# Attention and gated MLP on one core: chunk 0's rows in another order, one load on another queue, and a new instruction planner

## The chip, the core and the metric

The kernel runs on one core of a Trainium2 chip. A core has a matrix engine (TensorE, in the profile PE, with its weight loads as PEld), three engines for elementwise work (VectorE or DVE, ScalarE or ACT, GpSimd or POOL) and SyncE (SP), which only issues transfers. Sixteen DMA engines move data between the DRAM and the on-chip memory. A transfer is issued on the queue of SP, ACT or POOL and all of them share those sixteen. Each engine works through its own instructions in order; an instruction that waits for another engine or for a transfer holds up all that stand behind it. Matmul results land in eight PSUM banks, from which DVE or ACT must read them before the bank can be used again.

The metric is the device time of one execution in microseconds. Before the change it was 222.25 us, the median of three runs (221.79, 222.25, 227.55).

## The reference

Two stages follow each other. Decayed linear attention over q, k, v of 4 batches, 8 heads, 768 positions and 64 channels:

```python
for b in range(nb):                                   # blocks of 64 positions
    intra = einsum('bhic,bhjc->bhij', qb, kb) * Dmask # Dmask[i,j] = lam**(i-j) for i >= j
    intra = einsum('bhij,bhjd->bhid', intra, vb)
    inter = einsum('bhid,bhde->bhie', qb * lam_pow, kv_state)
    out[:, :, sl] = intra + inter
    kv_state = lam_block * kv_state + einsum('bhsd,bhse->bhde', kb * rev_pow, vb)
```

Its output, as x with 3072 rows (batch and position) and 512 columns (head and channel), goes through a layer with a periodic gate, and the result is stored as float32, [3072, 512]:

```python
h = x @ w_in                    # [3072, 2048]
s = sin(alpha * h)
g = h + s * s / (alpha + 1e-9)
return g @ w_out                # [3072, 512]
```

## The kernel before

**Attention.** The kernel uses 24 blocks of 128 rows, six to a batch. Instead of a mask with decay, queries and keys are scaled by powers of lam (tiles Lq, Lp, Lk), so that a 0/1 mask is left. For each block: load q, k, v; scale q and k to bf16 (qk); cast v; transpose the scaled q and k (tile qkT); scores S (L635) and their masked copy Sm on DVE (L646); state Z (L671), copied out as Zd or Zc; output O from the state (L708, L721) and from the scores (L730); copy of O to xT, transposed activations for the next stage (L740). Blocks 0 to 11 are transposed on PE (Q at L561, K at L583, T at L543) and copied out by DVE or ACT; from block 12 on, SP issues a DMA transpose (L534).

**Mixed rows.** Blocks 0 to 3 are loaded so that a partition gets neighbouring rows (q in fours, k and v in pairs), which makes longer runs in DRAM. O of these blocks comes out with its 128 rows sorted by their place within four. The copy to xT (L740) puts them back in order: `xT[...].rearrange("p a (x t) -> p a t x", t=nq)`, a strided write.

**The dense layer.** Rows are worked on in six chunks of 512. `unit_A` (four matmuls of 512 columns, L779) and `unit_A2` (eight of 256, L813) compute h for a slice of 128 columns into a bank. ACT takes the sine (t, L789 or L823), POOL or ACT squares it (u, L794, L793, L828, L827), DVE forms u * rinv + h (gT, L796 or L831). `unit_B` (four matmuls, L844) adds up four slices of the second product; after four of them ACT copies the bank to osb (L857) and a transfer stores 128 rows (L859). Chunk 0's four stores go out on SP's queue, all others but the very last on ACT's.

**Start.** `lam` (decay rates) and `alphaT` are loaded on ACT's queue; SP issues q, k, v of blocks 0 to 3 and the first slices of w_in. ACT computes ln(lam) (L460), then the powers (L464 to L470), with a table load ahead of each new kind of function, and then loads the table for the sine (L471). alpha is transposed by PE (L474), copied by DVE (L476), and aeps and rinv follow at once on DVE. Until the first unit_A, filler matmuls on a constant tile (`spin`, L935, 512 columns) stand in PE's gaps. Of the first scalings, DVE does two products of q and one of k, POOL two of q (L495) and three of k (L513).

**The planner.** The order of instructions on each engine is not written by hand. The kernel records operations with an engine (or a choice of engines), a planned duration, and what they read and write; `_Plan._order` then lays them out in planned time, and `emit` issues them with semaphore waits. `_order` always takes the operation that can start first, by planned durations; a fixed 0.2 us (LAT) is added between engines, PE may choose among the next 40 of its operations and SP none. A transfer is planned with an issue time, a time on the wire and a latency; `_transfers` shares the wire among the queues, and `_settle` repeats the plan eight times with the landings of the last pass and keeps the one that agrees best. `P.lead` moves attention pieces ahead in the priorities.

SP's order around chunk 0's stores: loads of blocks 10 and 11, the four stores, loads of blocks 12 and 13, loads of block 14, transpose of block 12, the loads of k and v of block 15, transpose of block 13, and so on.

Of the kernel before, what the change touches and what calls it, by code (L numbers as in the profile page):

```python
# [5 lines left out]
ALU = mybir.AluOpType  # L6
# [7 lines left out]
class _Op:  # L14


    def __init__(self, eng, emit, dur, reads, writes, dma, after, issue, lat, runs=64):
        self.eng, self.emit, self.dur = eng, emit, dur
        self.given = eng
        self.issue, self.lat, self.runs = issue, lat, runs  # L20
        self.lead = 0
# [11 lines left out]
class _Plan:  # L33

    AHEAD = {"PE": 40, "SP": 1}
    SLACK = 0.3  # L40
    EARLY = 0.0, 0.0

    LAT = 0.2
# [10 lines left out]
    def op(self, eng, emit, dur, reads=(), writes=(), dma=None, after=(), issue=0.4, lat=2.6, runs=64):  # L54
# [14 lines left out]
        o.deps.discard(o)  # L69
        o.lead = self.lead  # L70
# [4 lines left out]
    def _transfers(order):  # L75
# [5 lines left out]
        left = {e: [[o.start + 0.8, o.runs, o.dur / o.runs, o] for o in sorted(q, key=lambda o: o.start)]  # L81
# [19 lines left out]
    def _settle(self):  # L101

        filler, lands, best = self.filler, {}, None
        for _ in range(8):
            self.filler = filler
            for o in self.ops:
                o.eng, o.start, o.done = o.given, None, None
            order = self._order(lands)
            new = self._transfers(order)
            off = sum(abs(t - o.done) for o, t in new.items())  # L110
            state = [(o, o.eng, o.start, o.done) for o in order]
            if best is None or off < best[0]:
                best = off, order, state
# [5 lines left out]
    def _order(self, lands):  # L119
        index = {o: i - o.lead for i, o in enumerate(self.ops)}  # L120
        left = {}
        for o in self.ops:
            left.setdefault(o.eng if isinstance(o.eng, str) else "any", []).append(o)
        fixed = {e: left.pop(e, []) for e in ("PE", "SP")}
        free = [o for e in left for o in left[e]]
        clock = {e: 0.8 for e in ("PE", "SP", "ACT", "DVE", "POOL")}
        wire = 0.0
        port = 0.0
        order = []

        def ready(o):
            t = 0.0
            for d in o.deps:
                if d.done is None:
                    return None
                t = max(t, d.done + (0.0 if d.eng == o.eng else self.LAT))
            return t

        while fixed["PE"] or fixed["SP"] or free:
            best = None  # L140
            for e in ("PE", "SP"):
                can = []
                for o in fixed[e][:self.AHEAD[e]]:
                    r = ready(o)
                    if r is not None:
                        can.append((max(r, clock[e]), index[o], o, e, o.dur))
                if can:
                    soon = min(c[0] for c in can)
                    soon += self.EARLY[1] if e == "PE" and soon < self.EARLY[0] else self.SLACK
                    c = min((c for c in can if c[0] <= soon), key=lambda c: c[1])  # L150
                    if best is None or c[:2] < best[:2]:
                        best = c
            for o in free:
                r = ready(o)
                if r is None:
                    continue
                if o.port:
                    r = max(r, port)
                if isinstance(o.eng, str):
                    c = (max(r, clock[o.eng]), index[o], o, o.eng, o.dur)  # L160
                else:
                    _, e, d = min((max(r, clock[e]) + d + late, e, d) for e, d, late in o.eng)
                    c = (max(r, clock[e]), index[o], o, e, d)
                if best is None or c[:2] < best[:2]:
                    best = c
            t, _, o, e, dur = best
            if e == "PE" and self.filler is not None:
                emit, reads, last = self.filler
                if last.start is not None:
                    self.filler = None  # L170
                else:
                    deps = [self.writer[b] for b in reads]
                    at = max([clock["PE"]] + [d.done + self.LAT if d.done is not None else t for d in deps])
                    n = int((t - at) / 0.4)
                    if n > 0:
                        f = _Op("PE", lambda h, n=n: emit(h, n), 0.4 * n, tuple(reads), (), None, (), 0, 0)
                        f.deps = set(deps)
                        f.start, f.done = at, at + 0.4 * n
                        order.append(f)
            if isinstance(o.eng, str):  # L180
                (fixed[e] if e in fixed else free).remove(o)
            else:
                free.remove(o)
                o.eng = e
            o.start = t
            if o.dma is not None:
                clock[e] = t + o.issue
                wire = max(wire, t + 0.8) + dur
                o.done = max(t + 0.8 + o.dur + o.lat, lands[o]) if o in lands else wire + o.lat
            else:  # L190
                clock[e] = o.done = t + dur
                if o.port and e != "ACT":
                    port = o.done
            order.append(o)
        return order
# [48 lines left out]
def bass_lightning_attn__then__act_snake_kernel(  # L244
# [34 lines left out]
    QD = ((0, 0), (1, 0))  # L279

    es = contextlib.ExitStack()
    with es:
# [51 lines left out]
        def _(_unused_eng):  # L334
# [562 lines left out]
            for i in range(1, 4):  # L897
                load_w1(i, [last["v32", 1]])
# [137 lines left out]
```

## Time and profile before

| | us |
|---|---|
| median of three runs | 222.25 |
| the three runs | 221.79, 222.25, 227.55 |
| the profiled execution | 221.06 |
| its span | 219.2 |
| PE, ACT, DVE, POOL busy | 207.6, 157.2, 123.0, 96.0 |
| filler matmuls L935 | 8.4 |
| first matmul of the dense layer (L813) | starts at 20.58 |
| last store lands | end of the span |

The times of the runs are those of executions without the profiler; the profile is of one execution, and its own time is the span plus the parts ahead of it and behind it. A line such as `L646 DVE TENSOR_TENSOR Sm<-bank,mask 128x1024 bf16<-128x1024 f32 x24 | 29.1, 1222 | 10.4` reads: line, engine, operation, output and inputs, shape and type, number of instructions, then their time in us and the mean of one in ns, and the idle time of the engine just ahead of them. In rows by time the first two numbers are the start and the duration in us; "x4" says that four instructions are merged. SPq and ACTq are issues of transfers on the queues of SP and ACT. "To landing" is the time from the start of an issue to the last byte. Matmuls overlap, so a matmul of 512 columns is listed with 0.38 us, while four of them follow each other in 0.86 us. The "DMA" row gives the mean busy share of the sixteen DMA engines in 40 slices; in the tables by stage it can pass 1, as one engine can have more than one packet under way.

### The profile page before, as it was taken

What the parts mean: (1) busy time and instruction counts of PE and PEld (TensorE: products, weight loads), DVE (VectorE), ACT (ScalarE), POOL (GpSimd) and SP (SyncE); (2) the same over time, 40 slices, a digit from 0 to 9 for tenths busy, and PEclk for the clock granted to TensorE, in tenths of its full rate; (3) what the DMA queues carried; (4) which work ended last, traced back from release to release, by engine and by line L of the source; (5) the groups of instructions that cost most, each with busy time, mean ns of one, the idle gap of its engine ahead of it and who ended that gap; (6) DMA issues with size and microseconds to landing.
All of it is one profiled execution on the core that took longest, in us unless ns stands there. A gap on an engine that the chain in (4) does not pass through costs nothing.

```text
span 219.2 us, 4238 instructions
## 1 busy us (share of the span) xinstructions
PE 207.6 (95%) x1714; PEld 112.2 (51%) x1739; DVE 123.0 (56%) x185; ACT 157.2 (72%) x279; POOL 96.0 (44%) x110
## 2 busy tenths in 40 slices
PE   7787999999999979999999999999999999999995
PEld 2365544446577656555445444545544444444454
DVE  4688675444878858957564556545464544444100
ACT  4577986364988888969798787878778677777221
POOL 7793677756886777574551533011001011110100
PEclk9999999999999999999999999999999999999999
DMA  4999999999999999999999560110011011101212
GB/s 132 310 314 210 207 215 214 220 219 250 235 314 221 240 186 271 162 290 179 281 254 208 123 144 10 41 48 35 16 48 51 0 48 48 51 0 48 87 58 96
DMA packets 78499, 33.31 MB, mean 152 GB/s; under 512 B 55296, under 2 KB 75536, under 8 KB 78480
## 3 DMA queue, kind: packets, MB, share of 16 engines
q1 hardware_dynamic: 71728, 24.25, 53.4%
q0 software_dynamic: 3696, 3.67, 10.1%
q10 hardware_dynamic: 3056, 5.13, 6.5%
q8 instruction: 13, 0.21, 0.4%
q14 instruction: 6, 0.05, 0.1%
HBM read 27.28 MB, written 6.29 MB: 153 GB/s over the span
## 4 chain that ended last, share of the span: by engine, by line
PE 66%; DMA 20%; POOL 5%; ACT 3%; DVE 2%; issue 2%; SPq 1%; ACTq 0%; POOLq 0%
PE bank L844 33%; PE bank L779 22%; DMA k<-in_k_dram 10%; PE bank L813 4%; DMA w<-in_moe_w_in_dram 4%; DMA q<-in_q_dram 3%; DMA v<-in_v_dram 3%; PE bank L730 2%; PE bank L635 2%; POOL qk L513 2%; SPq L346 1%; POOL u L794 1%; POOL qk L505 1%; PE bank L708 1%; DVE gT L831 1%
## 5 line engine op out<-in xcount | busy, mean ns | idle before, releaser
L844 PE MATMUL bank<-w,gT 128*128 128x512 bf16 (+1 forms) x382 | 91.3, 371 | 1.8 <-issue 1.3
L796 DVE SCALAR_TENSOR_TENSOR gT<-u,rinv,bank 128x512 bf16<-128x512 bf16 x74 | 54.6, 745 | 52.2 <-ACT u L793 30.0
L779 PE MATMUL bank<-xT,w 128*128 128x512 bf16 x290 | 73.1, 379 | 0.6 <-issue 0.2
L789 ACT ACTIVATE t<-bank,alpha 128x512 bf16<-128x512 f32 x74 | 50.5, 686 | 23.2 <-PE bank L779 23.1
L794 POOL TENSOR_TENSOR u<-t 128x512 bf16<-128x512 bf16 x26 | 26.9, 1039 | 86.6 <-ACT t L789 84.7
L844 PEld LDWEIGHTS bank<-w,gT 128*128 128x128 bf16 x400 | 37.9, 98 | 39.5
L779 PEld LDWEIGHTS bank<-xT,w 128*128 128x128 bf16 x296 | 28.5, 98 | 34.1 <-ACT xT L740 0.6
L646 DVE TENSOR_TENSOR Sm<-bank,mask 128x1024 bf16<-128x1024 f32 x24 | 29.1, 1222 | 10.4 <-PE bank L671 7.1
L793 ACT ACTIVATE u<-t 128x512 bf16<-128x512 bf16 x48 | 30.0, 628 | 1.3
L857 ACT COPY osb<-bank 128x512 f32<-128x512 f32 (+1 forms) x25 | 14.2, 571 | 14.3 <-PE bank L844 14.2
L505 POOL TENSOR_TENSOR qk<-q,Lq 128x512 bf16<-128x512 f32 x20 | 20.4, 1042 | 8.2 <-DMA q<-in_q_dram 8.2
L813 PE MATMUL bank<-xT,w 128*128 128x256 bf16 x176 | 22.5, 273 | 1.5 <-DVE gT L831 1.5
L525 POOL TENSOR_TENSOR qk<-k,Lk 128x512 bf16<-128x512 f32 x20 | 20.8, 1042 | 2.6 <-DMA k<-in_k_dram 2.5
L823 ACT ACTIVATE t<-bank,alpha 128x256 bf16<-128x256 f32 x44 | 18.5, 474 | 4.5 <-PE bank L813 4.1
L831 DVE SCALAR_TENSOR_TENSOR gT<-u,rinv,bank 128x256 bf16<-128x256 bf16 x44 | 18.8, 474 | 4.9 <-ACT u L827 2.6
L813 PEld LDWEIGHTS bank<-xT,w 128*128 128x128 bf16 x176 | 16.1, 98 | 4.8 <-DVE gT L831 2.4
L740 ACT CAST xT<-bank 128x512 bf16<-128x512 f32 (+1 forms) x18 | 14.4, 799 | 3.6 <-PE bank L671 2.2
L528 ACT CAST v<-v 128x512 bf16<-128x512 f32 x16 | 9.8, 614 | 4.3 <-DMA v<-in_v_dram 4.3
L828 POOL TENSOR_TENSOR u<-t 128x512 bf16<-128x512 bf16 x9 | 9.3, 1038 | 6.5 <-ACT t L823 6.5
L730 PE MATMUL bank<-Sm,v 128*64 128x128 bf16 (+1 forms) x224 | 11.0, 224 | 0.6 <-DVE Sm L646 0.3
L635 PE MATMUL bank<-qkT 64*128 64x128 bf16 (+1 forms) x224 | 9.6, 219 | 0.3 <-ACT qkT L594 0.2
L935 PE MATMUL bank<-idle 128*128 128x512 bf16 x21 | 8.4, 540 | 1.6 <-DVE idle L441 1.5
(68 smaller groups left out, 125.7 us busy)
## 6 DMA issues: line engine op xcount, KB each, us to landing
q<-in_q_dram SPq DMA_DIRECT2D x12, 512.0 KB, 5.6
k<-in_k_dram SPq DMA_DIRECT2D x24, 256.0 KB, 5.5
v<-in_v_dram SPq DMA_DIRECT2D x24, 256.0 KB, 5.7
out_dram<-osb ACTq DMA_DIRECT2D x19, 256.0 KB, 2.0
w<-in_moe_w_out_dram POOLq DMA_DIRECT2D x4, 512.0 KB, 12.7
w<-in_moe_w_in_dram POOLq DMA_DIRECT2D x3, 512.0 KB, 8.0
ws<-in_moe_w_in_dram SPq DMA_DIRECT2D x2, 512.0 KB, 6.2
out_dram<-osb SPq DMA_DIRECT2D x4, 256.0 KB, 4.2
```

The source lines that it names most:

```text
L505: lambda e, a=a: e.tensor_tensor(qk2[:, j:j + 2, 4 * a:4 * a + 4, :], q32[:, jq, 4 * a:4 * a + 4, :, :].rearrange("p h t d -> p t h d"), b ...
L525: lambda e: e.tensor_tensor(qk2[:, j, H:2 * H, :], block32(k32, jl), lk, ALU.mult), 1.05,
L646: op("DVE", lambda e: e.tensor_tensor(Sm[js][:, :, :], banks[:, 512 * b0:512 * b0 + 1024].rearrange("p (c i) -> p c i", i=128), bass.AP(ma ...
L779: ins = e.matmul(ps[hb][:, c0:c1], w1[:, kc, 128 * m:128 * (m + 1)], xT[x][:, kc, c0:c1], start=(kc == 0 and c0 == lo), stop=(kc == NKC - ...
L789: op("ACT", lambda e: e.activation(t16[ju][:, w], ps[hb][:, w], ACTF.Sin, scale=alpha[:, m:m + 1]), 0.69 * f, [bank(hb), "alpha"], [("t16" ...
L793: lambda e: (e.activation(u16[ju][:, w], t16[ju][:, w], ACTF.Square) if e is nc.scalar else e.tensor_tensor(u16[ju][:, w], t16[ju][:, w], ...
L794: e.tensor_tensor(u16[ju][:, w], t16[ju][:, w], t16[ju][:, w], ALU.mult)), 0,
L796: op("DVE", lambda e: e.scalar_tensor_tensor(out=gT[g][:, m, w], in0=u16[ju][:, w], scalar=rinv[:, m:m + 1], in1=ps[hb][:, w], op0=ALU.mul ...
L813: ins = e.matmul(ps[hb][:, 256 * i:256 * i + 256], w1[:, kc, 128 * (m + i):128 * (m + i + 1)], xT[x][:, kc, lo:lo + 256], start=(kc == 0 a ...
L823: op("ACT", lambda e, i=i: e.activation(t16[ju][:, 256 * i:256 * i + 256], ps[hb][:, 256 * i:256 * i + 256], ACTF.Sin, scale=alpha[:, m + ...
L831: op("DVE", lambda e, i=i: e.scalar_tensor_tensor(out=gT[g][:, m + i, lo:lo + 256], in0=u16[ju][:, 256 * i:256 * i + 256], scalar=rinv[:, ...
L844: ins = e.matmul(ps[ob][:, w], gT[g][:, m, 128 * s4:128 * (s4 + 1)], w2[:, m, w], start=(m == 0), stop=(m == NM - 1),)
```

## The change

1. **Rows of blocks 0 to 3.** The copy to xT writes them in the order in which they lie in the bank, a contiguous write; the rows of a block are put in order by the store of chunk 0, whose pattern in DRAM is then 4 x 32 rows of 512 instead of 128 rows of 512.
2. **Start.** lam is loaded on SP's queue, ahead of q. alpha is copied from its bank by ACT instead of DVE; aeps and rinv are recorded later. DVE does all four products of q and three of the four of k; POOL does one of k. Of the four value casts, ACT does that of blocks 2 and 3, first half, instead of blocks 0 and 1, first half. The filler matmul has 256 columns instead of 512, and scores of block 3 are recorded ahead of the output of block 0.
3. **Planner.** `_order` is rewritten: each engine has a window within which the priority decides (WINDOW), an overlap of consecutive instructions (PIPE), a delay after another engine's work (HOP, and DRAIN after PE), and fillers have two durations. Many planned durations and transfer times are new. Engines and orders of most of the program change with it.

```diff
-    AHEAD = {"PE": 40, "SP": 1}
-    SLACK = 0.3
-    EARLY = 0.0, 0.0
-    LAT = 0.2
+    AHEAD = 40
+    WINDOW = {"PE": 0.3, "ACT": 0.1, "DVE": 0.1, "POOL": 0.1}
+    PIPE = {"ACT": 0.11, "DVE": 0.09, "POOL": 0.045, "PE": 0.0}
+    HOP = {"PE": 0.055, "ACT": 0.035, "DVE": 0.035, "POOL": 0.075, "SP": 0.1}
+    DRAIN = 0.085
+    MOVES = ()
+    SPIN = 0.22, 0.11, 7.4
...
-    QD = ((0, 0), (1, 0))
+    QD = ((0, 0), (0, 2), (1, 0), (1, 2))
...
-            load(lam_bc[:, :], ..., "lam", 0.1, "lam", "ACT", runs=1)
+            load(lam_bc[:, :], ..., "lam", 0.1, "lam", "SP", lat=1.3, runs=1)
...
-            op("DVE", lambda e: e.tensor_copy(alpha[:, :], ps[4][:, 0:NM]), 0.2, [bank(4)], ["alpha"])
-            op("DVE", lambda e: e.tensor_scalar_add(aeps[:, :], alpha[:, :], 1e-9), 0.2, ["alpha"], ["aeps"])
-            op("DVE", lambda e: e.reciprocal(rinv[:, :], aeps[:, :]), 0.2, ["aeps"], ["rinv"])
+            op("ACT", lambda e: e.copy(alpha[:, :], ps[4][:, 0:NM]), 0.2, [bank(4)], ["alpha"])
...
-                        eng, dur = (("DVE", 0.9) if a == 0 else ("POOL", 1.05)) if s == 0 else ("POOL", 1.05)
+                        eng, dur = ("DVE", 0.66) if s + a < 3 else ("POOL", 1.05)
...
-                        op("ACT" if s + a == 0 else "POOL", ...
+                        op("ACT" if s and not a else "POOL", ...
...
-                        xT[c % RX][:, a0:a1, BL * i4:BL * (i4 + 1)].rearrange("p a (x t) -> p a t x", t=nq),
+                        xT[c % RX][:, a0:a1, BL * i4:BL * (i4 + 1)].rearrange(
+                            "p a (x t) -> p a t x" if s >= 4 else "p a (t x) -> p a t x", t=nq),
...
-                    op(eng, lambda e: e.dma_start(out[row:row + 128, w], osb[jo][:, w]), 0.75,
+                    rows = out[row:row + 128, w] if c else bass.AP(out.tensor, row * DM + lo, [[DM, 4], [4 * DM, 32], [1, hi - lo]])
+                    op(eng, lambda e: e.dma_start(rows, osb[jo][:, w]), 0.75,
...
-            piece_O(0, 3)
             piece_S(3, 5, 6)
+            piece_O(0, 3)
...
-                    ins = e.matmul(ps[0][:, :], idle[:, 0:128], idle[:, :])
+                    ins = e.matmul(ps[0][:, 0:256], idle[:, 0:128], idle[:, :])
```

The new loop that takes the next operation:

```python
for e, c in per.items():                       # c: (earliest start, priority, op, duration)
    if not c:
        continue
    soon = min(x[0] for x in c) + self.WINDOW.get(e, 0.0)
    x = min((x for x in c if x[0] <= soon), key=lambda x: (x[1], num[x[2]]))
    if best is None or x[0] < best[0]:
        best = x[0], x[2], e, x[3]
```

More of the change, by code (lines that the diff above doesn't have):

```diff
@@ L101, in _settle @@
     def _settle(self):
[L103 to L111, printed above, removed]
+        prio = {o: i - o.lead for i, o in enumerate(self.ops)}
+        for at, width, kind, by in self.MOVES:
+            for o in self.ops[at:at + width]:
+                if (kind == "all" and o.given != "SP") or o.given == kind or (kind == "any" and not isinstance(o.given, str)):
+                    prio[o] += by
+        lands, best = {}, None
+        for _ in range(10):
+            order, new, off = self._pass(prio, lands)
             if best is None or off < best[0]:
-                best = off, order, state
+                best = off, order, [(o, o.eng, o.start, o.done) for o in order]
+            if off < 0.5:
+                break
             lands = new
@@ L117, in _settle, with _pass @@
         return best[1]
[L119 to L121 removed]
+    def _pass(self, prio, lands):
         for o in self.ops:
[L123 to L168 removed]
@@ L194, in _order @@
             order.append(o)
+            can.discard(o)
+            left -= 1
+            for s in after.get(o, ()):
+                waits[s] -= 1
+                if not waits[s]:
+                    can.add(s)
         return order
```

166 lines of the change are left out of this document (110 added, 56 removed).

## The prediction

> **What bounds the kernel now.** I read the busy shares and the slices first, then the list of waits for TensorE (PE) alone, then the order of time on single engines around the places where PE stops. The page of the profile:
>
> ```profile
> PE 207.6 (95%) x1714; PEld 112.2 (51%) x1739; DVE 123.0 (56%) x185; ACT 157.2 (72%) x279; POOL 96.0 (44%) x110
> ...
> DMA  4999999999999999999999560110011011101212
> ...
> q1 hardware_dynamic: 71728, 24.25, 53.4%
> ...
> q10 hardware_dynamic: 3056, 5.13, 6.5%
> ```
>
> PE is busy for 95% of the span, but its first 20 us are partly filler matmuls (L935), and the DMA engines are full until about 118 us. So there are two limits: PE from the first real matmul of the dense part (20.58 us) on, and before 118 us the transfers that feed it. The waits of PE (engine, line, what it waited for: total us, times, longest):
>
> ```profile
> PE bank L813 <- DVE gT L831: 1.5, 2, 1.2
> ...
> PE bank L543 <- POOL qk L525: 0.5, 1, 0.5
> ```
>
> Between 20.58 us and the end these are nearly all that PE loses: 0.48 us at 41.27 (keys of block 4 not yet scaled, their load landed at 40.01), 0.26 at 59.09 and 1.20 at 79.71 (gate values late, behind a value cast that waited on ACT for its load), 0.16 at 97.95. Together 2.1 us: a better order can win no more there. The third view is the SP queue and the attention of block 12, the first block whose transposes are DMAs (start us, us, engine, line):
>
> ```profile
> 59.39 2.83 SPq L859 DMA_DIRECT2D out_dram<-osb  x4
> 62.26 0.84 SPq L346 DMA_DIRECT2D q<-in_q_dram  x1
> ...
> 73.09 3.31 SPq L534 DMA_TRANSPOSE qkT<-qk  x1
> ...
> 77.69 2.27 SPq L534 DMA_TRANSPOSE qkT<-qk  x1
> ```
> ```profile
> 85.86 0.40 PE L635 MATMUL bank<-qkT 64*128 64x128 bf16 x8
> ```
>
> The four stores of chunk 0 stand in the same queue right ahead of the loads of blocks 12 and 13 (from 62.26). The transposes of those blocks go out at 73.09 and 77.69; the second landed 4.4 us later, at 82.1. The scores of block 12 need both and start at 85.86: 3.7 us of slack.
>
> **Part by part: the start.** Decay rates on SP: one more issue of 0.44 us with its gap (0.47) ahead of all loads, so k lands 0.47 later (9.19 to 9.66); between 0 and 0.47, I take 0.47 and cost it at nothing, because the products below start later still (without that cover, +0.47). The rates themselves landed 3.5 us after their issue; from SP, with nothing ahead, between 1.7 (the shortest landing in the trace, the last store) and 3.5; I take 3.5, because they start the engines' work together with the same loads. More weighs that the copy of alpha is now on ACT, ahead of the table load for the exponentials:
>
> ```profile
> 4.59 1.28 ACT L464 ACT_TABLE_LOAD   x1
> 5.88 0.23 ACT L464 ACTIVATE Lq<-lnL 128x32 f32<-128x32 f32 x1
> ...
> 15.79 1.31 ACT L740 CAST xT<-bank 128x512 bf16<-128x512 f32 x1 [0.23 <-PE bank L730]
> ```
>
> alphaT, first on its queue, lands 3.5 us (lam's time there) to 4.8 us (its own) after 0.81, at 4.3 to 5.6. PE transposes it behind 18 half-size fillers (half of 0.43 us each, from 1.5: 5.3), 0.23 us, then the copy, 0.2: ACT is free at 5.8 to 6.1 instead of 4.57, and Lq is there at 7.3 to 7.6 instead of 6.11. Queued behind this wait: the four exponentials, and all scaling. DVE now does four q and three k products, 0.66 us each (L495 on DVE) where POOL took 1.29 and 1.23. From 7.4 the sixth ends at 11.4, against 11.04 in before, so the first scores start at 12.6 instead of 12.24: +0.4. If POOL's one k product runs beside a DVE one, that costs up to 0.9 more (the DVE one of before that ran beside POOL took 1.52). Sin's table load hides in ACT's idle time, and the changed value casts (0.61 us on either engine) wait for later loads.
> The four mask products (4.62 us in a row) shift with the scores. Against that, the contiguous xT copies: 1.31 us becomes 0.74 (a later L740 copy of that size, at 74.31), and two of them stand in ACT's chain Zd, xT, Zd that ends at O(3): up to 1.1 back. The dense part starts at 19.9 to 21.0; I take 20.3, **-0.3 us**. Smaller filler and idle tiles, and the move of aeps and rinv, change nothing on the path: DVE waits for Lq there anyway.
>
> **The planner.** I counted, in the two programs' orders on PE, how many dense units (four 512-column or eight 256-column matmuls, 0.864 us) precede each attention piece. Block 4's key transposes move from 22 to 25, blocks 8 to 11 by 3 to 4 units back: the waits at 41.27 and 79.71 lose their cause. I take 1.0 of the 2.1 us, since new small waits of that kind are as likely as old ones go: **-1.0**; bounds 0 and -2.1. Against the stream the scores of block 12 come *forward* from 56 to 54, block 14 from 67 to 65, block 16 from 79 to 75; from 85 on the orders agree. Forward by 1.73 us leaves block 12 2.0 us of slack, and block 14 1.7 (transposes landed 93.2, use at 96.61). 22 squares move from POOL to ACT (61 to 83), 0.63 us each, 13.9 us on an engine with 62 us idle; hidden while ACT keeps up (second rival).
>
> **The store.** Chunk 0's rows are permuted by the store: its DRAM pattern changes from 128 rows to 4 x 32 rows. The packet count says how a transfer is dealt out: q10's 3056 packets are 20 stores of 128 rows, 128 for lam, 16 for alphaT, and 352 = 22 transfers x 16. So every transfer there closed with 16 packets, which I read as 16 shares, one for each DMA engine, alphaT with its 16 rows among them. Every pattern in before has 128 or 16 as its outermost size; the new one has 4. I forecast that the outermost size sets the shares: **four engines instead of 16**. The trace can't decide it: 16 rows fit "always 16" as well.
> Price: q10 moved 5.13 MB in 6.5% of 16 x 219.2 us, 22.5 GB/s for one engine. Four stores of 256 KB are 64 KB per engine on 16 (2.9 us), but 256 KB on each of four (11.6 us). Those four engines fall 8.7 us behind, and each later load on this queue, spread over all, ends with them. Between 64 and 74 us the DMA share is 0.84 to 1.09, against about 1.25 when full: some 2.2 us to catch up (five windows of 2 us). So the transposes of block 13 land 6.5 us late, at 88.6 (bounds: 5.0, if the engines go at up to 27 GB/s as the last stores suggest, 256 KB in 2.0 us and 128 KB in 1.7; 8.7 without catching up). PE comes to the scores of block 12 at 85.86 - 1.73 - 1.3 = 82.8 and stands for 5.8 us; everything behind it on PE waits too, the second half of the dense work with it. Blocks 14 and 16 then come after their data, and the loss stays. What is gained ahead only lengthens this wait, so the net loss is lateness less slack, 6.5 - 2.0 = 4.5; down to 1.7, if the first transpose, held at 73.09 by the queue and not by its data (1.3 us), hides that much.
> The Trainium skill, page "DMA: Bandwidth & Descriptors", section "Why a DMA increments its semaphore by 16 and not by 1", speaks against this change: by it the hardware queues take the largest number up to 16 that divides the slowest dimension of both sides. By that rule it is 4 here; no run here shows it yet.
> A stop of over 5 us can also cost speed behind it. At the start fillers of 512 columns stand 0.43 us apart until 7.04, later such matmuls 0.216: a cold spell of 5.9 us, up to 3 us lost. After the 1.20 us wait at 79.71 nothing was slower. I take 0, nearest to the waits seen in mid-kernel, and keep 3.
> By the Trainium skill's "TensorE: Matmul & The Clock Gate", Part 1, an idle window of about 3.4 us halves the clock and a busy one restores it; by that rule the sum would be 1.7 us higher.
>
> **Sum.** 221.06 (span 219.2 and 1.86 around it) - 0.3 - 1.0 + 5.8 = 225.6. The two lower runs shown (221.79, 222.25) lie 0.7 and 1.2 above the profiled one; with 0.9 the forecast is **226.5 us**.
>
> **Rivals.** *All 16 engines carry the store* (not slower): then transposes land at 82.1, ahead of PE at 82.8, and the gains stay: 221.06 - 1.3 = 219.8, as timed 220.6 (219.4 to 221.9); for it, that all 22 transfers of q10 closed with 16 packets. The landing at 82.1 also caps it: beyond 2.0 us of gain PE waits again. *ACT becomes the bound*: between 80 and 120 us ACT is busy 33.7 of 40 us; some five squares more there at 0.57 us (two in a row took 1.14 at 24.95) make 91%, and in-order waits for loads stand among them. If all of that reaches PE: 221.06 - 0.3 + 2.8 = 223.6, as timed 224.5. Against it, ACT waits 23 us for PE at L779. *The change wins nothing at its start* (exponentials late by 1.5, a DVE and POOL collision): +0.4, inside the ranges.
>
> **Chances.** Forecast 0.58, sixteen engines 0.30, ACT 0.12. The forecast's own range is 223.7 to 229.5 (222.8 to 227.6 by the bounds, 0.9 added, some of the 3 us of cold clock); to leave out under 2 in 10 the range takes in the second case: 219.6 to 229.5. Two per cent, about what a measurement of this kernel tells from no change, ends at 217.8 and 226.7. Slower: somewhat under half of the forecast and a bit of ACT, 0.30. Faster: a tenth of the sixteen engines, and planner's luck, 0.04. Same: 0.66.
>
> **What would show it.** q10 must have 2912 packets; q1 71872 with 16 closing packets for each store, 71824 with four. The four stores land in 4.3 to 5.4 us now; with four engines after 8 us and more. PE idles 4 to 7 us at L654 near 83 us, waiting for qkT. Lq near 7.4, the dense part from 20.3, xT copies at 0.74 show the start. Wrong it would be if the stores land as before, or if SP's loads of block 12 do not queue behind them.

## The result and the profile after

| | before | after |
|---|---|---|
| median of the runs | 222.25 us (three runs, as above) | 229.66 us (four runs: 228.13, 229.46, 229.85, 232.41) |
| ratio of after to before, 95% interval | | 1.0294 [1.0227, 1.0361] |
| a second set of after, six runs | 222.87 us (11 runs) | 229.75 us, ratio 1.031 [1.0251, 1.0369] |
| the profiled execution, its span | 221.06, 219.2 us | 232.41, 230.5 us |

The change makes the kernel 3% slower; the forecast was 226.5 us, about 2%. A fourth execution of before took 358.71 us and is left out of its median. The profiled execution of after is the longest of its four, and that of before (221.06) is shorter than all its timed ones, so the traces lie 11.35 us apart where the medians lie 7.4 apart. Ratios here and below leave out single executions that are more than 1.5% above the fastest of their kernel; medians do not.

From the page of after: the clock granted to PE in 40 slices, the busy share of the DMA engines, and the queues (packets, MB, share):

```profile
PEclk9997699999999999599999999999999999999999
DMA  4999999999744899999999618101100111011122
...
q1 hardware_dynamic: 71824, 24.26, 48.7%
...
q10 hardware_dynamic: 2912, 5.12, 6.8%
```

q1 has 71824 packets, the number foretold for four engines (71872 would have been 16). Where before's DMA engines were full, in the slices from 58 to 81 us, they drop to four to eight tenths. And PE, at full clock throughout in before, runs at half clock in two places. The SP queue of after (start, duration), and the waits of PE (total us, times, longest):

```profile
60.15 5.78 SPq L880 DMA_DIRECT2D out_dram<-osb  x4
65.97 0.51 SPq L368 DMA_DIRECT2D q<-in_q_dram  x1
66.53 4.56 SPq L368 DMA_DIRECT2D k<-in_k_dram  x1
71.13 3.62 SPq L368 DMA_DIRECT2D v<-in_v_dram  x1
...
80.91 2.75 SPq L553 DMA_TRANSPOSE qkT<-qk  x1
...
84.95 3.29 SPq L553 DMA_TRANSPOSE qkT<-qk  x1
```
```profile
PE bank L654 <- DMA qkT<-qk: 5.2, 1, 5.2
```

The loads of block 12 stand behind the stores (q for 12 and 13 at 65.97, then k and v of 12). Their issues, 0.8 to 2.6 us each in before, now take up to 4.6 us. The transposes go out at 80.91 and 84.95 instead of 73.09 and 77.69. The second takes 7.5 us to land, at 92.5 (4.4 us, at 82.1, in before). The chain that ended last (start, us, what) runs through just these pieces:

```profile
65.97 10.38 DMA q<-in_q_dram
...
84.95 7.53 DMA qkT<-qk
```

PE stops for 5.2 us ahead of the scores of block 12 (L654), and then works at half clock. The table by stage gives the busy time of each engine, and at the end of the row the clock, the DMA share and GB/s:

```profile
92.53 0.61 PE L654 MATMUL bank<-qkT 64*128 64x128 bf16 x8 [5.20 <-DMA qkT<-qk]
93.07 3.60 PE L833 MATMUL bank<-xT,w 128*128 128x256 bf16 x16
```
```profile
90.00:95.00 5.00, 2.47 (x18) 1.73 (x19) 1.23 (x1) 0.16 (x2) 0.87 (x1) 0.65 1.21 247
95.00:100.00 5.00, 5.00 (x21) 2.50 (x20) 1.22 (x3) 3.89 (x8) 2.17 (x3) 0.67 1.26 233
```

Sixteen matmuls of 256 columns took 3.60 us, against 2.02 for the first sixteen of the dense part in before. By the two rows the half clock lasts (0.35 + 0.33) x 2 x 5 = 6.8 us, to 98.3, and behind the wait it costs (98.3 - 92.5) / 2 = 2.9 us.

The books: block 12's scores start at 92.53. In before they started at 85.86, and the new order has them two dense units (1.73 us) earlier, so they are 8.4 us late. With 2.9 us of clock that makes 11.3, the whole difference of the two profiled executions (232.41 - 221.06 = 11.35). What PE did ahead of that wait is hidden in it.

### The profile page after: what moved, and what is told of

It reads as the page before. It is cut to its first block, busy times and chain, and to the rows that moved or that the text cites. A ratio compares the mean times of both kernels' runs of the same rounds, so it can differ in the third digit from the quotient of the medians.

```text
span 230.5 us, 4320 instructions
## 1 busy us (share of the span) xinstructions
PE 216.3 (94%) x1769; PEld 118.5 (51%) x1769; DVE 119.8 (52%) x182; ACT 167.9 (73%) x307; POOL 69.2 (30%) x85
## 3 DMA queue, kind: packets, MB, share of 16 engines
q1 hardware_dynamic: 71824, 24.26, 48.7%
## 4 chain that ended last, share of the span: by engine, by line
PE 77%; DMA 10%; DVE 5%; ACT 4%; POOL 2%; issue 1%; SPq 0%
PE bank L864 34%; PE bank L799 28%; DMA q<-in_q_dram 7%; PE bank L833 4%; DMA qkT<-qk 3%; PE bank L749 3%; PE bank L654 2%; PE bank L959 2%; POOL qk L524 2%; DVE Sm L665 2%; PE bank L727 1%; DVE qk L532 1%; ACT t L843 1%; DVE gT L851 1%; PE bank L690 1%
## 5 line engine op out<-in xcount | busy, mean ns | idle before, releaser
L864 PE MATMUL bank<-w,gT 128*128 128x512 bf16 (+1 forms) x400 | 95.1, 371 | 0.0
L799 PE MATMUL bank<-xT,w 128*128 128x512 bf16 x296 | 76.0, 386 | 0.0
L799 PEld LDWEIGHTS bank<-xT,w 128*128 128x128 bf16 x296 | 29.3, 99 | 35.3 <-issue 1.4
L813 ACT ACTIVATE u<-t 128x512 bf16<-128x512 bf16 x67 | 42.0, 629 | 2.0
L524 POOL TENSOR_TENSOR qk<-q,Lq 128x512 bf16<-128x512 f32 x20 | 20.4, 1042 | 20.9 <-DMA q<-in_q_dram 20.9
L833 PE MATMUL bank<-xT,w 128*128 128x256 bf16 x176 | 25.7, 300 | 0.5 <-DVE gT L851 0.3
L833 PEld LDWEIGHTS bank<-xT,w 128*128 128x128 bf16 x176 | 17.5, 107 | 5.4 <-DVE gT L851 1.7
L654 PE MATMUL bank<-qkT 64*128 64x128 bf16 (+1 forms) x224 | 9.6, 222 | 6.6 <-DMA qkT<-qk 5.2
L759 ACT CAST xT<-bank 128x512 bf16<-128x512 f32 (+1 forms) x19 | 13.0, 685 | 1.7 <-PE bank L749 1.7
L654 PEld LDWEIGHTS bank<-qkT 64*128 64x128 bf16 (+1 forms) x224 | 5.7, 99 | 11.6 <-DMA qkT<-qk 5.4
L749 PE MATMUL bank<-Sm,v 128*64 128x128 bf16 (+1 forms) x224 | 11.5, 233 | 0.0
L848 POOL TENSOR_TENSOR u<-t 128x512 bf16<-128x512 bf16 x6 | 6.2, 1038 | 16.3 <-ACT t L843 16.3
L814 POOL TENSOR_TENSOR u<-t 128x512 bf16<-128x512 bf16 x7 | 7.3, 1037 | 12.0 <-ACT t L809 12.0
L547 ACT CAST v<-v 128x512 bf16<-128x512 f32 x15 | 9.0, 615 | 2.5 <-DMA v<-in_v_dram 2.4
```

The lines of the kernel that those rows point to most:

```text
L524: lambda e, a=a: e.tensor_tensor(qk2[:, j:j + 2, 4 * a:4 * a + 4, :], q32[:, jq, 4 * a:4 * a + 4, :, :].rearrange("p h t d -> p t h d"), b ...
L654: ins = e.matmul(ps[(b0, b1)[h]][x, 128 * jp:128 * (jp + 1)].rearrange("p (t x) -> p t x", t=nq), qkT[r, jt, 4 + jp, x], qkT[r, jq:jq + nq ...
L799: ins = e.matmul(ps[hb][:, c0:c1], w1[:, kc, 128 * m:128 * (m + 1)], xT[x][:, kc, c0:c1], start=(kc == 0 and c0 == lo), stop=(kc == NKC - ...
L813: lambda e: (e.activation(u16[ju][:, w], t16[ju][:, w], ACTF.Square) if e is nc.scalar else e.tensor_tensor(u16[ju][:, w], t16[ju][:, w], ...
L833: ins = e.matmul(ps[hb][:, 256 * i:256 * i + 256], w1[:, kc, 128 * (m + i):128 * (m + i + 1)], xT[x][:, kc, lo:lo + 256], start=(kc == 0 a ...
L864: ins = e.matmul(ps[ob][:, w], gT[g][:, m, 128 * s4:128 * (s4 + 1)], w2[:, m, w], start=(m == 0), stop=(m == NM - 1),)
```

## The experiments

Where an edit names "the changed kernel", the rest is as in after.

**1. Sixteen and eight engines.** The same four stores, from the same tiles, in descriptors of the same size; only the pattern in DRAM differs (and with it the order of chunk 0's rows in the result, which these two kernels leave mixed).

```diff
-  [[DM, 4], [4 * DM, 32], [1, hi - lo]]
+  [[DM, 16], [16 * DM, 8], [1, hi - lo]]      # and, in the second, [[DM, 8], [8 * DM, 16], ...]
```

> The changed kernel, but chunk 0's four stores have the DRAM pattern 16 x 8 rows in place of 4 x 32; the same bytes in descriptors of the same size, the order of all instructions is unchanged. (The rows of chunk 0 end up in another order than the reference's; nothing else differs.) Theory (few engines carry the 4 x 32 store): the four stores land in 4 to 6 us from their issue, q1 has 48 packets more (71872), the transposes of block 13 land near 82 us, PE has no wait over 2 us for qkT and no spell at half clock near 90 us; time 219.4 to 223 us. Rival (the new order of the planner, or the start, makes the loss): same time as the changed kernel, 227 us or more.

> The changed kernel with the pattern 8 x 16 rows for chunk 0's four stores. (Rows of chunk 0 in another order than the reference's; nothing else differs.) Theory (the outermost size sets the number of engines): eight engines, q1 71840 packets (16 more than the changed kernel), the stores take twice as long as with 16, about 5.8 us on the wire; the transposes of block 13 land 3 to 5 us later than with 16 engines, PE waits 0.5 to 3 us for qkT at the scores of block 12, too short for a spell at half clock; 221 to 224 us. Rival A (the count of shares is 4 or 16 only): as the changed kernel or as 16 x 8. Rival B (the planner): 227 us or more.

Measured: 16 x 8 rows 223.41 us, just above the range expected, ratio to before 1.0026 [0.9984, 1.0069]; 8 x 16 rows 224.04 us, at the upper end of its range, 1.0012 [0.9969, 1.0055]. (Before itself had a median of 223.35 in these 25 runs.) The queue, and the second transpose, for 16 engines:

```profile
q1 hardware_dynamic: 71872, 24.26, 53.7%
```
```profile
64.44 0.59 SPq L368 DMA_DIRECT2D q<-in_q_dram  x1
...
78.89 2.46 SPq L553 DMA_TRANSPOSE qkT<-qk  x1
```

and for eight, with PE's wait:

```profile
q1 hardware_dynamic: 71840, 24.26, 51.5%
```
```profile
86.32 0.40 PE L654 MATMUL bank<-qkT 64*128 64x128 bf16 x8 [2.34 <-DMA qkT<-qk]
```

Packet counts of 71872, 71840 and 71824 are four stores with 16, 8 and 4 closing packets. The q load behind the stores landed 4.9, 7.8 and 10.4 us after its issue. From the first store's issue to the landing of block 13's transposes it takes 23.8, 26.4 and 32.3 us. One thing was not as expected: behind the 2.3 us wait of the second kernel the clock was at half for some 3 us too (0.84 from 80 to 90 us). The times do not show what that wait and that spell cost: the intervals of 16 and 8 engines overlap almost wholly. So the outermost size of the pattern sets the number of engines, and that alone carries the loss: the changed kernel with its planner and its start, but a store on 16 engines, is level with before. This settles the cause. It also agrees with the rule in the Trainium skill, "DMA: Bandwidth & Descriptors", section "Why a DMA increments its semaphore by 16 and not by 1", which before's trace could not decide.

**2. Part 1 alone, and all but part 1.** Contiguous copies and the 4 x 32 store in the kernel before; and the changed kernel with strided copies and the plain store of 128 rows.

```diff
 part 1 alone, in the kernel before:
-  .rearrange("p a (x t) -> p a t x", t=nq)
+  .rearrange("p a (x t) -> p a t x" if s >= 4 else "p a (t x) -> p a t x", t=nq)
-  out[row:row + 128, w]
+  out[row:row + 128, w] if c else bass.AP(out.tensor, row * DM + lo, [[DM, 4], [4 * DM, 32], [1, hi - lo]])
 all but part 1: the same two edits the other way round, in the changed kernel
```

> The kernel before with part 1 alone: contiguous copies to xT and the 4 x 32 store of chunk 0; start, planner and order as before. Theory: the transposes of block 13 land 9 to 11 us late against 3.7 us of slack; PE waits 5 to 7 us for qkT at the scores of block 12 and runs at half clock for some us behind it; 227 to 232 us. Rival (the loss needs the new plan): within 2% of the kernel before.

> The changed kernel without part 1: strided copies to xT for blocks 0 to 3 and the plain store of 128 rows; start and planner as changed, the same order of instructions. Theory: no wait for qkT at block 12; 219.4 to 223 us, and by its difference to 16 x 8 rows (within 0.7 us) the contiguous copies are worth little. Rival (contiguous copies are worth the 1.1 us of the prediction): 1 us longer than 16 x 8. Rival (planner): 227 us or more.

Measured: part 1 alone 232.96 us, 1.0421 [1.0337, 1.0506], 1.0 above the range expected; all but part 1 224.72 us, 1.0069 [1.0033, 1.0104], 1.7 above its range. The latter is also 1.3 us longer than 16 x 8 rows in the median, as the rival of useful contiguous copies had it, but the intervals overlap. Part 1 alone does damage under the old plan too. There PE's wait has another name, and ACT shows its cause:

```profile
PE bank L813 <- DVE gT L831: 6.5, 2, 6.2
```
```profile
88.52 0.62 ACT L528 CAST v<-v 128x512 bf16<-128x512 f32 x1 [6.46 <-DMA v<-in_v_dram]
```

ACT stands for 6.46 us at a value cast whose load is late; the squares behind it, the gate values and PE wait with it. From the first store's issue to block 13's transposes it takes 28.9 us here, against 22.7 in before. In this execution the stores were also issued 4.3 us later than in before (63.67 against 59.39), because the start was late for a reason of its own (experiment 6; the dense part starts at 25.10 instead of 20.58). So not all of the 4% is part 1's; whether the start was late in the other three executions is not known.

**3. The same rows in order, on 16 engines.** Each store is issued as four stores of 32 rows.

```diff
+  [e.dma_start(bass.AP(out.tensor, (row + t) * DM + lo, [[4 * DM, 32], [1, hi - lo]]),
+               osb[jo][32 * t:32 * t + 32, w]) for t in range(4)]
```

> The changed kernel with each of chunk 0's four stores issued as four stores of 32 rows (DRAM pattern 32 rows, every fourth one), so the rows come out in the reference's order and the outermost size is 32. Order of all other instructions as in the changed kernel; SP issues 12 transfers more. Theory (the outermost size sets the number of engines, at most 16): 16 shares each, q1 72064 packets (71824 - 4 x 4 + 16 x 16), no wait for qkT over 2 us at block 12; the 12 issues at 0.4 to 0.6 us delay SP by 5 to 7 us, of which the queue's own backlog hides most: 221.5 to 225 us. Rival (a transfer of 32 rows out of 32 partitions is slow for another reason, as many partitions as rows): 227 us or more.

Measured: 228.41 us, 1.0247 [1.0168, 1.0325], where 221.5 to 225 was expected. The packets are as foretold (72064), so each part went to 16 engines, and each landed in 1.7 us (median). But:

```profile
59.84 9.46 SPq L883 DMA_DIRECT2D out_dram<-osb  x16
69.34 0.44 SPq L369 DMA_DIRECT2D q<-in_q_dram  x1
```
```profile
PE bank L655 <- DMA qkT<-qk: 3.4, 1, 3.4
```

Sixteen issues at 0.59 us hold SP for 9.5 us, and the q load goes out at 69.34 instead of 64.44. The time is in the rival's range, but not for the rival's reason, a slow transfer. The expectation that the queue's backlog hides the issues was wrong: with 16 engines there is little backlog, and the 4.9 us reach PE as 3.4 us of wait and a stretch at lower clock.

**4. The stop and the clock.** The changed kernel with matmuls on the idle tile between block 12's other waits and its wait for the transposes, so that PE is busy while it waits: 44 of them, then 28 beside a second set of the changed kernel itself.

```diff
+  for _ in range(28): e.matmul(ps[1][:, 0:256], idle[:, 0:128], idle[:, :])   # ahead of the wait for qkT
```

> The changed kernel with 44 matmuls of 256 columns on the constant tile (0.108 us each, 4.8 us) between block 12's waits on other engines and its wait for the transposes: PE is busy while it waits. Theory (the stop itself causes the spell at half clock behind it): the wait for qkT shrinks to under 1 us, no spell at half clock near 91 us, time 1.7 to 3 us below the changed kernel's: 225.5 to 228 us. Rival (the spell has another cause, or the granted clock in the records says nothing of matmul times): within 1 us of the changed kernel's 229.7.

> The changed kernel itself, unchanged, beside the others of this set: 228 to 232 us, with the mean granted clock between 0.97 and 0.985. Every theory expects this; it is what the kernel with 28 fillers is compared with.

> As the one with 44 matmuls ahead of block 12's wait, with 28 (3.0 us), so that they end before the transposes land. Theory (the stop costs clock behind it, 1.7 us for one window at half speed): 1 to 2.5 us below the changed kernel beside it, 227 to 229 us, wait for qkT 1 to 3 us, no spell at half clock behind it. Rival (the half-speed spells move elsewhere or cost nothing that the wall of the loads doesn't hide): within 0.7 us of the changed kernel beside it.

Measured: 44 fillers 229.76 us, 1.0297 [1.0218, 1.0376], no gain, as the rival had it. They ended at 93.7 us, after the transposes had landed (86.11 + 6.9 = 93.0). With 28 fillers 228.66 us, 1.0264 [1.0209, 1.032], beside the changed kernel at 229.75, 1.031 [1.0251, 1.0369]: 1.1 us less, with overlapping intervals. The traces are clearer than the times. The changed kernel, second set, then 28 fillers:

```profile
91.94 0.61 PE L654 MATMUL bank<-qkT 64*128 64x128 bf16 x8 [4.42 <-DMA qkT<-qk]
```
```profile
90.00:95.00 5.00, 3.06 (x20) 2.10 (x21) 1.22 (x1) 1.15 (x3) 1.27 (x2) 0.50 1.21 256
```
```profile
90.10 0.40 PE L666 MATMUL bank<-qkT 64*128 64x128 bf16 x8 [0.98 <-DMA qkT<-qk]
```
```profile
90.00:95.00 5.00, 4.84 (x36) 3.00 (x38) 2.23 (x4) 3.45 (x8) 2.73 (x3) 1.00 1.28 246
```

With a busy PE no half clock follows the wait (with 44 fillers one spell lies ahead of them, 0.86 from 80 to 85 us and 0.80 from 85 to 90, behind a wait of 3.4 us for xT), and from block 12's scores to the end of the span it is 135.3 us (225.4 - 90.10; with 44 fillers 229.0 - 93.68 = 135.3 as well), against 137.3 (229.2 - 91.94) and 138.0 (230.5 - 92.53) without. In these traces the stop costs 2.0 and 2.7 us behind itself; the times show 1.1 of it, not clear of the noise. The Trainium skill, "TensorE: Matmul & The Clock Gate", Part 1, has the clock halved after an idle window of about 3.4 us; the 1.7 us estimated from it for one window is below both measured values, two windows (3.4) are above. Both fit if a part of the spell passed while PE stood: in after it lasted 6.8 us and began at 91.5, and PE started again at 92.5.

**5. Planner and start.** Part 3 alone (parts 1 and 2 taken back); and all but part 1, with alpha's copy back on DVE. The edit of the second:

```diff
-  op("ACT", lambda e: e.copy(alpha[:, :], ps[4][:, 0:NM]), 0.2, [bank(4)], ["alpha"])
+  op("DVE", lambda e: e.tensor_copy(alpha[:, :], ps[4][:, 0:NM]), 0.2, [bank(4)], ["alpha"])
```

> The kernel before with part 3 alone: the new planner and its durations, with the rows, the store, the load of lam, alpha's copy, the first products and casts and the fillers of 512 columns as before. Theory (the prediction's term): 1.0 us faster than the kernel before, bounds 0 and 2.1: ratio 0.990 to 1.0. Rival (the planner wins nothing, since what it saves at 41 and 79 us comes back as new small waits): ratio 1.0 to 1.006; then the loss of the kernel without part 1 (ratio 1.0069) is in the start if this one is at 1.0, in the planner if it is at 1.006.

> The changed kernel without part 1, and with alpha's copy on DVE as before, so that ACT goes from the logarithm straight to the exponentials; the rest of the start as changed. Theory (the copy ahead of the exponentials costs the start 1.1 us): Lq by 5.6 to 6.0 us in place of 7.24, the first scores at 11.0 to 11.5 in place of 12.03, the dense part from 19.9 to 20.4 in place of 20.9, time 0.5 to 1.0 us below the kernel without part 1 (224.7): 223.5 to 224.3. Rival (the loads of k set the start, and the copy is hidden): first scores within 0.3 us of 12.03 and the same time.

Measured: the planner alone 1.0026 [0.9956, 1.0096] from three executions (223.0 to 224.6), in the rival's range; seven others took 229.5 to 231.5, which experiment 6 takes up. With alpha's copy on DVE 223.45 us, 1.0014 [0.9976, 1.0052], 1.3 us under the kernel with the copy on ACT (224.72), again with overlapping intervals. Its start:

```profile
5.93 0.23 ACT L486 ACTIVATE Lq<-lnL 128x32 f32<-128x32 f32 x1 [0.69 <-DVE lnL L484]
```
```profile
10.95 0.69 PE L654 MATMUL bank<-qkT 64*64 64x128 bf16 x32
...
20.81 3.20 PE L833 MATMUL bank<-xT,w 128*128 128x256 bf16 x16
```

Lq is there at 6.2 instead of 7.24, and the first scores come at 10.95 instead of 12.03: the copy did cost the start 1.1 us. The dense part, though, starts at 20.81 against 20.91. So the theory held for the first scores and failed for the dense part. PE ran at half clock from 16.6 us on and waited 0.74 us for Zd. Where the 1.3 us of the median come from is not shown by this trace.

**6. lam's queue.** In the run of part 1 alone, with lam on ACT's queue as in before, lam landed late:

```profile
6.87 0.21 ACT L460 ACTIVATE lnlam<-lam_bc 128x8 f32<-128x8 f32 x1 [3.74 <-DMA lam_bc<-in_lam_dram]
```

In before's profile this instruction starts at 4.36. So two kernels got lam on SP's queue, ahead of q, and nothing else: the kernel before, and the planner alone.

```diff
-  load(lam_bc[:, :], ..., "lam", 0.1, "lam", "ACT", ...)
+  load(lam_bc[:, :], ..., "lam", 0.1, "lam", "SP", ...)
```

> The kernel before with one edit: lam is loaded on SP's queue ahead of q. Theory (in some executions lam, small and on another queue, lands late behind the first loads, at 6.8 us in the run of part 1 alone against 4.3, and the start waits): the spread of the kernel before (221.5 to 226.4) narrows at its upper end, to 221.5 to 224; the ratio of the medians 0.993 to 1.0. Rival (the spread is the clock's alone): same median and spread as the kernel before.

> The new planner alone, with one edit: lam on SP's queue ahead of q. The planner alone gave 223.0 to 224.6 in three runs and 229.5 to 231.5 in seven. Theory (lam landing late is what its slow runs share): all runs at 222.5 to 225. Rival (the slow runs come from another wait of the new plan): some runs at 229 us or more again.

Measured, with the kernel before beside them in the same set: before took 221.5 to 223.0 us in 13 executions and 224.2 to 226.8 in 18. With lam on SP it took 221.4 to 222.1 in eight of ten, 223.7 and 224.9 in the others (median 221.79, ratio 0.9986 [0.9958, 1.0014]). The planner with lam on SP took 220.8 to 224.6 in all ten (222.20, 0.9982 [0.9938, 1.0027]), where without it seven of ten were near 230. The long executions go with lam on ACT's queue. With the kernel before that is shown side by side; the planner's two sets were taken on different chips. That lam lands late in the long executions is seen in one trace, of another kernel, and is only argued for the rest.

**7. The store out of the way.** Chunk 0's result is copied to ws, which is free after the start, and stored behind the last transpose.

```diff
-  op("ACT", lambda e: e.copy(osb[jo][:, w], ps[ob][:, w]), 0.59, [bank(ob)], [("osb", jo)])
+  op("ACT", lambda e: e.copy(ws[:, s4, :], ps[ob][:, :]), 0.59, [bank(ob)], ...)    # chunk 0 only
...
             assert block == NBLK + 1
+            for st in stores: st("SP")       # taken away ahead of blocks 8 to 11
```

> The changed kernel with chunk 0's result copied to the tile ws (free after the start) and its four stores, still of 4 x 32 rows on four engines, issued on SP's queue behind the last transpose, when the DMA engines are nearly idle. Theory (the few-engine store costs only what stands behind it in a full stretch): q1 keeps 71824 packets, the four stores are slow (8 us or more) and cost nothing, the transposes of block 13 land by 80 us, no wait for qkT at block 12; as 16 x 8 rows (223.4) or up to 1 us less: 222.3 to 223.6. Rival (stores on few engines cost PE or ACT time wherever they stand): 225 us or more.

> As the one with late stores, and alpha's copy on DVE. Theory (the two gains are in different places and add): 1.2 us below the one with late stores, 221.2 to 222.6, ratio to the kernel before 0.990 to 0.997. Rival (the gain at the start is eaten by a later wall, such as the loads of the dense weights or block 4's): same as with late stores, 222.3 to 223.6.

> The new planner with lam on SP's queue, and chunk 0's result stored late from ws with the plain pattern of 128 rows; no part 1, the start otherwise as before. Theory (nothing of the store was on the path at 16 engines): as the new planner with lam on SP, 221.5 to 223. Rival (loads of blocks 12 and 13 that land earlier help): 220 to 221.5.

> As that, with part 1's contiguous copies and 4 x 32 stores, issued late: the same order of instructions on PE. Theory (the contiguous copies shorten the chain into the dense part by up to 1.1 us): 0.5 to 1.2 us below the one without them, 220.3 to 222.5, and below both given kernels. Rival (the mask products on DVE set that chain, the copies are hidden): within 0.3 us of it.

Measured: the changed kernel with late stores 222.73 us, 1.0002 [0.996, 1.0044]. Its stores still go to four engines (q1 71824), but now stand where nothing is behind them:

```profile
76.86 2.16 SPq L553 DMA_TRANSPOSE qkT<-qk  x1
...
131.61 3.47 SPq L884 DMA_DIRECT2D out_dram<-ws  x4
```

Block 13's transposes land at 81.4, a little later than expected, and no wait for qkT is left. So the few-engine store is cheap in itself and dear only for the queue behind it. With alpha's copy on DVE as well it was not faster but 223.46 us, 1.0048 [1.0011, 1.0085]; the expected sum of the two gains failed and the rival's range holds. The first scores came at 10.95 here too, and then PE stood:

```profile
18.29 0.53 PE L690 MATMUL bank<-v,qk 64*64 64x64 bf16 x12 [1.93 <-issue]
```

On the planner with lam on SP, late stores without and with part 1 gave 221.32 us, 0.9894 [0.9818, 0.997], and 220.21 us, 0.9893 [0.9831, 0.9955]. Both beat both given kernels, by 1% (less than the two per cent that the prediction asks for) and by 4%. The medians lie 1.1 us apart, as expected, but the ratios do not differ at all, so the times leave open what contiguous copies are worth. The traces say more. PE's waits between the first scores and the dense part, first without and then with contiguous copies:

```profile
PE bank L692 <- ACT Zd L702: 0.8, 1, 0.8
PE bank L729 <- ACT Zd L702: 0.6, 1, 0.6
```
```profile
PE bank L751 <- issue: 1.8, 1, 1.8
```

The two waits for Zd, which ACT makes behind its copies to xT, are gone, so in these traces the mask products did not set that chain. In their place PE stood 1.83 us in O(2) without a wait that the profile shows, and the dense part started at 21.32 instead of 21.53. That late stores gain beside the planner with lam alone (0.9982) fits the rival of earlier loads, but the intervals overlap.

## Why the prediction was right and wrong

- **The store on four engines**, the forecast's mechanism: right, by the packets and by experiment 1. "All 16 engines carry the store" is refuted; its 220.6 would have been 223.4. "ACT becomes the bound" showed nowhere: with 16 engines, the squares moved to ACT included, the kernel is level with before, and behind 21 us PE waits for ACT only twice, 0.2 us each.
- **The price of the lateness**, "8.7 us behind, minus 2.2 us to catch up, 6.5": block 13's transposes came 8.5 us late (32.3 against 23.8 with 16 engines), and by another route. The first load behind the stores, q, landed 16.2 us after the first store's issue, against 9.7 with 16 engines: 6.5 late at once, not 8.7. The first transposes landed 5.5 late, so next to nothing was caught up. The second ones were issued 5.5 late as well (24.8 against 19.3) but then took 7.5 us to land instead of 4.5. These 3.0 us are the first step that failed: the prediction kept before's 4.4 for this landing. Its 6.5 fits the loads by luck. In five traces (the changed kernel twice, both fillers, the split stores) 0.26 MB of the next store, on ACT's queue (q10), move inside this landing, and it took 5.6 to 7.5 us; in the thirteen others, where at most one packet of that store does, 4.1 to 5.7. That the store lengthens the landing was not tested. At eight engines the whole lateness was 2.6 (26.4 - 23.8), where the same row of before gives 2.9. The DMA share from 60 to 80 us shows that the loads caught up nothing though there was room:

```profile
60.00:70.00 10.00, 9.65 (x102) 6.60 (x94) 8.32 (x17) 8.91 (x21) 5.89 (x6) 1.00 0.58 159
70.00:80.00 10.00, 9.80 (x123) 7.11 (x120) 9.40 (x22) 9.52 (x21) 4.77 (x7) 1.00 0.62 158
```

  Before had 1.08 and 1.09 there. The other engines had room, but SP's queue didn't fill it: its k and v issues took 4.56 and 3.62 us. Room on engines was no room to catch up, as the work came through the queue that was late. Under the old plan q landed 7.0 us late and the whole stretch grew by 6.2 (28.9 against 22.7); the store on ACT's queue comes behind it there, and the second transposes landed in 4.2 us.
- **The stretch around the store**, costed at nothing: the stores started 0.8 later than in before (60.15 against 59.39), and from there on the new order takes 1.1 more even on 16 engines (23.8 against 22.7). Lateness 8.5 + 0.8 + 1.1 = 10.4, and 8.4 after the slack of 2.0, which was right, as were the two units by which block 12 moved.
- **The wait itself**, "5.8 us" near 83 us: 5.20, but from 87.3 on. PE came 4.5 us later than foretold and the transposes 3.9, so the number fits by luck.
- **The clock behind the stop**, "I take 0, and keep 3": 2.9 in the profiled execution, 2.0 in the second one. The row it leaned on, a wait of 1.20 us, was too short to tell; a stop of 5 us is another case.
- **The sum**: 225.6 was forecast for a profiled execution, and 232.4 came: 2.0 of lateness beyond the 6.5, 1.9 around the store and 2.9 of clock make the 6.8 between. These three terms were set too low or at nothing. That is the longest execution; the median, 229.66, lies 3.2 above the forecast and 0.16 above the range.
- **The start**, "-0.3 us, the dense part from 20.3": it started at 21.86 (20.94 in the second profile). Lq was foretold for 7.3 to 7.6 and came at 7.24, the first scores for 12.6 and came at 12.81; the xT copies went from 1.31 to 0.58. What failed is the step that these copies pull in the dense part. PE stood in the middle of Z(2) for 0.69 us without a wait that the profile shows, and a first spell at half clock followed; the pair of experiment 7 shows such a stop eat the gain of the copies alone. All of it lay ahead of the wait at block 12 and cost nothing at the end. Without part 1 it shows: 1.0069 against 0.9982 for the planner with lam on SP, some 1.9 us with intervals that do not meet ([1.0033, 1.0104], [0.9938, 1.0027]), of which alpha's copy may be 1.3. The mean clock goes with it: in the six kernels with the changed start that end near 223 us (experiments 1, 2, 5 and 7) none of 58 executions has a mean clock above 0.992, while 12 of the 22 with the old start, the new planner and lam on SP have 1.0. Which edit of the start lowers the clock was not tested.
- **The planner**, "-1.0": not found. The waits at 41.27 and 79.71 are gone in the kernel with 16 x 8 rows, but others came: 1.6 us behind 21 us (xT, Sm, gate values, t, osb) in place of 2.1. With lam on SP under both, the new planner stands at 0.9982 and the old one at 0.9986. Costing lam's new queue at nothing missed the best part of the change: with it before's long executions fell from 18 in 31 to 2 in 10.

## What to carry over

Read the outermost size of both sides of a store or load before you permute it: with 4 there, four engines carry it, and in a full stretch every transfer behind it on the queue waits; put such a transfer last, or where the queue has nothing behind it. Time that a queue loses need not be made up by idle engines (here 6.5 us late, and eight transfers on still 5.5), and the two long waits lowered the clock and cost 2.0 and 2.9 us more. A small load that everything waits for is worth a trial ahead of the big ones on their queue.

## What the runs showed of the hardware that was not expected

- Half clock also came without a long stop. From 16 to 20 us in after PE was busy for 3.0 of 4 us, and ran at half clock until 26.7:

```profile
16.00:18.00 2.00, 1.70 (x69) 1.39 (x59) 2.00 (x3) 1.55 (x5) 1.85 (x3) 1.00 1.21 226
18.00:20.00 2.00, 1.31 (x34) 1.05 (x36) 1.10 (x2) 1.17 (x3) 0.00 (x0) 0.95 1.24 205
20.00:25.00 5.00, 5.00 (x43) 3.57 (x40) 0.42 (x1) 2.22 (x6) 0.00 (x0) 0.50 1.24 207
```

  The longest stop there was 0.69 us. The Trainium skill's rule of an idle window of about 3.4 us ("TensorE: Matmul & The Clock Gate", Part 1), read as one unbroken stop, does not cover this, and the measurement decides; the same part also tells of many short stops that make the clock swing, which would fit. The mean clock of executions comes in steps of about 0.0077 (1.0, 0.992, 0.985, 0.977, 0.970); each is 3.4 us at half clock (0.0077 x 222 x 2), and one kernel varies by several steps from run to run.
- PE stopped with "issue" as the only cause between the first scores and the dense part: for 0.23 us in before, 0.69 in after, 1.86 in the run of part 1 alone, 1.83 and 1.93 in experiment 7. The DMA queues list an instruction queue (q8, 14 packets in after). In all fourteen traces with such a stop, the stop ends 2.2 to 2.7 us after the start of q8's first packet, and that packet lies anywhere from 14.8 us (alpha's copy on DVE) to 20.9 (part 1 alone). A late fetch of instructions behind full DMA engines would fit; it was not tested.
